# Seven products instead of eight in the first feed-forward matmul, and attention gathered between the pairs of batches

## Chip, cores, metric

One core of a Trainium2 chip. The metric is the device time of one execution in microseconds (us). Every run of a changed kernel was timed beside runs of the kernel before on the same chip. Each run has a state: slow, if it lies over 1.5% above the fastest of its kernel. A ratio is the mean time of one kernel's fast runs over that of the other's of the same rounds, so it is not quite the ratio of the medians that I quote.

## The reference, cut to what matters

```python
# q, k, v: 8 batches x 12 heads x 448 tokens x 64, values of size 0.1;  w_in 768x2048, w_out 2048x768
scores = scale * (q @ k.T) - log(S)
attn   = sigmoid(scores) @ v                       # x: 3584 tokens x 768, token-major
h      = x @ w_in                                  # first product
g      = h * sigmoid(h)
out    = g @ w_out                                 # second product
```

The kernel works in f16. A *unit* of attention is four heads of one batch, so there are 24 units, three for each batch, and unit n belongs to batch n // 3.

## The kernel before

TensorE's 128x128 array is used as four 64x64 tiles. A product runs in two lanes: its upper 64 rows (two matmuls, one for each half of the columns) and, some *chunks* later, its lower 64 rows, which add into the same PSUM bank. A chunk of one product's upper rows and a chunk of an earlier product's lower rows then fill the four tiles together: I call this a *four*. A queue (`fifo`) holds the lower rows still to be done. A marker makes the first lower matmul wait until the upper rows have left the bank.

```python
def lane_step(p=None, c=0):
    low = fifo.popleft() if lower_ready() else None     # lower rows of an earlier product, if due
    def go():
        if p:   p.last = p.mm(0, c)[-1]                 # two matmuls, upper rows
        if low: ... low[0].mm(1, low[1])                # two matmuls, lower rows
                # the first of them waits for low[0].last: "the upper rows have left the bank"
    ...
def emit(p, bank_id, deps):
    ff_wait(deps)                                       # may drain lower rows alone while it waits
    while len(fifo) > 2.5 * p.n:                        # p.n = 6 chunks in the first product,
        drain_one()                                     #       8 in the second
    for c in range(p.n):
        lane_step(p, c)
        ...  between()                                  # here a step of attention may be slipped in
```

The first product of a batch is 16 such products of 6 chunks, 448 columns wide (Python class `G1`, matmuls of L682). The second product was already done by seven products of quarters instead of eight (class `G2`, L808, with sums of quarters on DVE). Attention of units 8 to 23 needs k and q transposed; this is done by DMA:

```python
def transpose_dma(n):                                   # n >= 8; three DMA transposes for each unit
    pl.op("SP", 1200, ("trk", n), [("k", n)] + ([("S", n - NTR, NCH - 1)] if n >= NTR else []),
        lambda: nc.sync.dma_start_transpose(kT[n % NTR], xk[n % NX]), nbytes=1300)
    ...                                                 # two more for q; NTR = NX = 3 sets of buffers
```

`pl` models each engine's time and so fixes the order in which instructions are emitted. The order is fixed when the kernel is built.

## Time and profile before

| | kernel before |
|---|---|
| time, median of the four runs beside the changed kernel | 385.89 us (385.79 to 387.68) |
| span of the profiled run | 384.5 us |
| TensorE busy, mean granted clock | 366.5 us, 0.996 |
| DVE, ACT, GpSimd busy | 203.5, 232.6, 65.1 us |
| lost array time from first to last second product (83 to 379 us) | 12.1 us |

*Lost array time* is the length of a stretch less the matmuls that start in it at their full-rate cost, (columns/2.4 + 2.5) ns for four of them. The lines that carry the bound are in the prediction below.

### The profile page before, as it was taken

The page shows a single profiled execution, that of the slowest core. Times are in us where ns is not written, and L with a number is a line of the kernel's source. Part 1 is how long each engine was busy: PE and PEld are TensorE (multiplying, and loading weights), DVE is VectorE, ACT ScalarE, POOL GpSimd, SP SyncE. Part 2 cuts the span into 40 slices and gives each one's busy share as a digit, 9 for nine tenths or more (in the row PEclk, how much of TensorE's full clock was granted, in tenths as well). Part 3 has the DMA queues.
Part 4 walks back from the last instruction along what each step waited for, and adds up shares of the span by engine and source line. Part 5 has one row for each costly group of instructions (what it writes and reads, how often), then busy time and mean ns, then how long its engine had stood idle before and what let it go on. Part 6 is the DMA issues. An engine that isn't in the chain of part 4 may idle for free.

```text
span 384.5 us, 17994 instructions
## 1 busy us (share of the span) xinstructions
PE 366.5 (95%) x8024; PEld 307.8 (80%) x8024; DVE 203.5 (53%) x376; ACT 232.6 (60%) x506; POOL 65.1 (17%) x97
## 2 busy tenths in 40 slices
PE   7899899999998899989999999999999999999994
PEld 3477677888875599968889898988889898989773
DVE  3536699863444346454454646454654446465632
ACT  1994688568874666548648687776746864144010
POOL 9655102302222020211201222022000000000000
PEclk9999999999999999999999999999999999999998
DMA  8999995976999995975979988796692001410235
GB/s 104 198 209 204 209 208 77 145 94 96 161 185 173 148 119 98 188 122 93 144 112 179 178 113 122 146 157 83 117 155 66 2 3 44 95 34 2 66 75 115
DMA packets 80636, 46.51 MB, mean 121 GB/s; under 512 B 50608, under 2 KB 79792, under 8 KB 80560
## 3 DMA queue, kind: packets, MB, share of 16 engines
q0 software_dynamic: 25008, 22.81, 39.8%
q1 hardware_dynamic: 55552, 22.56, 34.0%
q8 instruction: 63, 1.03, 1.1%
q14 instruction: 13, 0.11, 0.1%
HBM read 45.61 MB, written 11.01 MB: 147 GB/s over the span
## 4 chain that ended last, share of the span: by engine, by line
PE 90%; issue 3%; ACT 2%; DMA 2%; POOL 1%; DVE 1%; POOLq 0%; ACTq 0%
PE ps L808 33%; PE ps L682 30%; PE ps L718 10%; PE ps L507 8%; PE ps L519 8%; ACT at L957 2%; DMA xk<-in_k_dram 2%; PE ps L465 1%; PE ps L990 1%; POOL xk L224 0%; POOL xq L233 0%; DVE qT L479 0%; DVE xt L979 0%; ACT sg L624 0%; POOL v L244 0%
## 5 line engine op out<-in xcount | busy, mean ns | idle before, releaser
L682 PE MATMUL ps<-xt,wi 64*64 64x448 f16 x2304 | 166.7, 349 | 4.9 <-issue 4.9
L550 ACT ACTIVATE at<-ps 128x448 f16<-128x448 f32 x252 | 122.0, 563 | 46.4 <-PE ps L507 40.3
L682 PEld LDWEIGHTS <-wi 64*64 64x64 f16 x2304 | 112.6, 107 | 19.3 <-issue 7.0
L629 DVE TENSOR_TENSOR gt<-ps,sg 128x448 f16<-128x448 f32 (+2 forms) x128 | 78.4, 621 | 71.6 <-ACT sg L624 71.2
L808 PE MATMUL ps<-wo,gt 64*64 64x384 f16 x1344 | 111.5, 323 | 0.3 <-issue 0.3
L808 PEld LDWEIGHTS <-gt 64*64 64x64 f16 x1792 | 97.8, 107 | 10.7 <-issue 1.9
L624 ACT ACTIVATE sg<-ps 128x448 f16<-128x448 f32 (+2 forms) x128 | 70.3, 554 | 54.3 <-PE ps L682 34.8
L808 PEld LDWEIGHTS <-gs 64*64 64x64 f16 x1344 | 78.1, 107 | 7.8 <-issue 0.3
L808 PE MATMUL ps<-so,gs 64*64 64x384 f16 x896 | 80.6, 323 | 0.0
L507 PE MATMUL ps<-qT,kT 64*64 64x448 f16 (+2 forms) x840 | 76.5, 318 | 2.2 <-ACT at L957 0.9
L822 DVE SCALAR_TENSOR_TENSOR us<-ps,us 128x384 f32<-128x384 f32 x70 | 38.7, 555 | 56.8 <-PE ps L808 46.9
L244 POOL DMA_DIRECT2D v<-in_v_dram x24 | 17.4, 723 | 206.7 <-PE ps L519 99.1
L808 PE MATMUL ps<-so,gt 64*64 64x384 f16 x448 | 45.4, 323 | 0.0
L957 ACT ACTIVATE at<-ps 128x512 f16<-128x512 f32 (+3 forms) x96 | 39.8, 555 | 9.2 <-PE ps L507 9.2
L507 PEld LDWEIGHTS <-kT 64*64 64x64 f16 x840 | 35.7, 108 | 11.9 <-issue 7.8
L808 PE MATMUL ps<-wo,gs 64*64 64x384 f16 x448 | 43.7, 323 | 0.0
L718 PE MATMUL ps<-xt,wi 128*128 128x256 f16 (+1 forms) x384 | 40.8, 260 | 1.1 <-issue 1.1
L519 PE MATMUL ps<-at,v 64*64 64x448 f16 (+2 forms) x840 | 40.9, 313 | 0.6 <-issue 0.6
L718 PEld LDWEIGHTS <-wi 128*128 128x128 f16 x384 | 33.1, 98 | 5.8 <-issue 2.5
L519 PEld LDWEIGHTS <-v 64*64 64x64 f16 x840 | 29.8, 107 | 6.2 <-issue 2.2
L829 ACT ACTIVATE us<-ps 128x384 f32<-128x384 f32 x28 | 14.0, 500 | 30.1 <-PE ps L808 30.0
L562 DVE TENSOR_SCALAR xt<-ps 128x448 f16<-128x448 f32 x36 | 20.8, 619 | 15.2 <-PE ps L519 14.5
(33 smaller groups left out, 150.0 us busy)
## 6 DMA issues: line engine op xcount, KB each, us to landing
out_dram<-us SPq DMA_DIRECT2D x112, 96.0 KB, 3.2
xk<-in_k_dram POOLq DMA_DIRECT2D x24, 224.0 KB, 5.6
v<-in_v_dram POOLq DMA_DIRECT2D x24, 224.0 KB, 4.9
xq<-in_q_dram POOLq DMA_DIRECT2D x21, 224.0 KB, 6.8
wo<-in_moe_w_out_dram POOLq DMA_DIRECT2D x4, 768.0 KB, 15.8
wi<-in_moe_w_in_dram POOLq DMA_DIRECT2D x8, 192.0 KB, 6.5
wi<-in_moe_w_in_dram POOLq DMA_DIRECT2D x4, 384.0 KB, 10.0
qT<-xq SPq DMA_TRANSPOSE x32, 4.6
```

The lines of the kernel that those rows point to most:

```text
L244: lambda: nc.gpsimd.dma_start(v16[n % NV], src(v, b, g)),
L507: nc.tensor.matmul(pt[r][64 * h : 64 * h + 64, lo : lo + (c1 - c0) * D], kT[n % NTR][64 * r : 64 * r + 64, i, 64 * h : 64 * h + 64], qT[n ...
L519: nc.tensor.matmul(pt[h][64 * j : 64 * j + 64, :N], v16[n % NV][64 * h : 64 * h + 64, j, c * D : (c + 1) * D], at[64 * h : 64 * h + 64, sl ...
L550: lambda r=r: nc.scalar.activation(at[:, sl, r], pt[r][:, :S], AF.Sigmoid, bias=NEG_LOG_S, scale=QKSCALE),
L562: lambda h=h: nc.vector.tensor_scalar_mul(x[:, 2 * g + h, :], pt[h][:, :S], SX), prio=-2,
L624: lambda: nc.scalar.activation(t[:, :ncol], src_, AF.Sigmoid, scale=ISX), prio=0,
L629: lambda: nc.vector.tensor_tensor(o, src_.rearrange("p (a t) -> p a t", a=nb), t[:, :ncol].rearrange("p (a t) -> p a t", a=nb), ALU.mult),
L682: nc.tensor.matmul(bank[64 * j : 64 * j + 64, z * N : z * N + N], wi[64 * h : 64 * h + 64, cc, f0 + 64 * j : f0 + 64 * j + 64], x[64 * h : ...
L718: nc.tensor.matmul(bank[:, z * N : z * N + N], wi[:, cc, fc * P : (fc + 1) * P], x[:, cc, self.c0 : self.c1], start=(cc == 0 and z == 0), ...
L808: nc.tensor.matmul(bank[64 * j : 64 * j + 64, :HE], lhs[64 * h : 64 * h + 64, c, 64 * j : 64 * j + 64], rhs[64 * h : 64 * h + 64, c, :], s ...
L822: lambda: nc.vector.scalar_tensor_tensor(o, bank[:, :HE], ISX, u, ALU.mult, ALU.add), prio=-2,
L957: lambda r=r, src_=src_: nc.scalar.activation(at[:, base : base + m, r, :N], src_, AF.Sigmoid, bias=NEG_LOG_S, scale=QKSCALE),
```

## The change

The intent is to do for batches 2 to 7 in the first product what the second already does: take two batches (a `Pair`) as a 2x2 of quarters and do seven products instead of eight, which takes 288 of 2304 matmuls off the array. The price is sums of x and w_in on DVE, combinations of PSUM banks on DVE through fp32 buffers (`us`), and copies on ACT. To pay for it, GpSimd multiplies h by its sigmoid for three of the four output quarters. SBUF has to be found for it all: later units get two sets of transposed buffers instead of three. A product in a pair has 3 chunks, and its lower rows follow after at most 7.5 chunks (15 before). Six units of attention stand in the first block of second products, then one in each of two pairs and five in each of two blocks. The core of the diff:

```diff
-        while len(fifo) > 2.5 * p.n:
+        while len(fifo) > (7.5 if p.n == NQ else 2.5 * p.n):
...
-    NTR = 3
-    NX = 3
+    def tring(n):
+        return n % 3 if n < NBIG else 3 if n in () else (0, 1, 0, 1, 0, 1)[n % 6]
...
-            pl.main += d
+            pl.main += d * (0.2 if p.n == NQ else 1.0)
...
+    class Pair:
+        def sums(self):                                  # four sums of x on DVE
+            tt(kk + (1,), d, lo, xs[:, 0], x12, x11, sub, -1)
+            ...
+        def run(self, j, n):                             # product n of 7, column block j of 8
+            lhs, rhs = {
+                1: (wi[:, k_lo, f_lo], x11), 2: (wi[:, k_hi, f_lo], x21), 6: (si[1][:, :, fl], xs[:, 1]),
+                7: (wi[:, k_lo, f_hi], x12), 5: (si[0][:, :, fl], xs[:, 0]), 4: (wi[:, k_hi, f_hi], xs[:, 2]),
+                3: (si[2][:, :, fl], x22),
+            }[n]
+            ...
+            def comb(o, i_, key, deps):
+                pl.op("DVE", 532, key, deps + u_free[o],
+                    lambda: nc.vector.scalar_tensor_tensor(us[o], bank[:, :S], ISX, us[i_], ALU.mult, ALU.add), prio=-2)
+            ...
+                pl.op("POOL", 100 + 2.0 * n_, keys[-1], [key + ("sg", lo)],
+                    lambda o=o, x_=x_: nc.gpsimd.tensor_tensor(o, x_, o, ALU.mult), prio=5)
...
-    blocks = [('p', [0, 1]), ('g', 2), ('p', [2, 3]), ('g', 3), ('p', [4, 5]), ('g', 4), ('p', [6]), ('g', 5), ('p', [7, 8]), ('g', 6), ('p', [9, 10]), ('g', 7), ('p', [11, 12, 13])]
+    blocks = [("p",[0,1,2]),("g",2),("p",[3,4,5]),("g",4),("p",[6,7,8]),("g",6),("p",[9,10,11,12,13])]
```

(The rest changes buffer indices and the guards that keep rings of buffers safe.) The `blocks` line is the coarse order. Before, second products ("p", one or two pairs of row groups) and batches of the first product ("g") alternate finely. After, blocks of 3, 3, 3 and 5 second products stand around the three pairs of batches. The weight of 0.2 makes the modelled pace of attention slow in the pairs, so that most of it falls into the blocks.

## The prediction

> **What bounds the kernel now.** I read the page first: engine shares, slices, groups. Columns of a group: count | busy us, mean ns of one | idle before it.
>
> ```profile
> PE 366.5 (95%) x8024; PEld 307.8 (80%) x8024; DVE 203.5 (53%) x376; ACT 232.6 (60%) x506; POOL 65.1 (17%) x97
> ...
> PE   7899899999998899989999999999999999999994
> ...
> PEclk9999999999999999999999999999999999999998
> DMA  8999995976999995975979988796692001410235
> ...
> L682 PE MATMUL ps<-xt,wi 64*64 64x448 f16 x2304 | 166.7, 349 | 4.9 <-issue 4.9
> ...
> L629 DVE TENSOR_TENSOR gt<-ps,sg 128x448 f16<-128x448 f32 (+2 forms) x128 | 78.4, 621 | 71.6 <-ACT sg L624 71.2
> L808 PE MATMUL ps<-wo,gt 64*64 64x384 f16 x1344 | 111.5, 323 | 0.3 <-issue 0.3
> L624 ACT ACTIVATE sg<-ps 128x448 f16<-128x448 f32 (+2 forms) x128 | 70.3, 554 | 54.3 <-PE ps L682 34.8
> ```
>
> TensorE is the bound, at full granted clock in all but the last slice. The idle columns of DVE and ACT name each other and PE: they wait, PE does not. Busy PE is not PE at its peak, so I next took the rate from the chain that ended last, where PE runs alone:
>
> ```profile
> 116.96 1.51 PE ps L682 x32
> ...
> 275.35 1.62 PE ps L808 x40
> ```
>
> Four 64x64 matmuls share the array, so a "four" of 448 columns costs 1.51/8 = 0.189 us and one of 384 columns 1.62/10 = 0.162 us. From the first L808 (83.1 us) to the last (379.2 us) the array then has to do: first product of batches 2 to 7, 2304/4 = 576 fours x 0.189 = 108.9; second product, 3136/4 = 784 x 0.1625 = 127.4; attention of units 6 to 23, 18 x 14 = 252 fours x 0.189 = 47.6. Sum 283.9 of 296.1 us: only 12 us are lost there. Busy time by stretch tells where:
>
> ```profile
> 112.00:143.00 31.00, 27.11 (x573) 20.89 (x569) 12.54 (x21) 18.74 (x40) 4.31 (x6) 1.00 1.07 147
> 143.00:318.00 175.00, 173.97 (x3865) 154.53 (x3860) 89.99 (x155) 118.26 (x253) 20.08 (x28) 1.00 0.71 116
> ```
>
> (length; busy PE, weight load, DVE, ACT, POOL; clock; DMA share; GB/s.) After 143 us PE is 99% busy; at 112 to 143 us it idles 3.9 us while the DMA share is over 1. What holds it there is seen in the SyncE queue, where issuing a transpose takes up to 4.31 us instead of about 1.2:
>
> ```profile
> 111.38 2.91 SPq L444 DMA_TRANSPOSE qT<-xq  x1
> 114.34 4.31 SPq L448 DMA_TRANSPOSE qT<-xq  x1
> ```
>
> So two limits: the array for most of the time, and the DMA that feeds attention, just after start-up.
>
> **What the Trainium skill says.** "TensorE: Matmul & The Clock Gate", section "Back-to-back issue gap": one warm matmul takes N/2.4 + 2.5 ns, 189.2 ns at N = 448 and 162.5 at 384; the trace agrees for a four. "VectorE: DVE Perf Modes", "The perf-mode tier table": a two-input operation that reads PSUM runs at one element per cycle; the trace agrees (467 ns for 448 elements at 0.96 GHz, shown as 621 ns with its fixed part). "GPSIMD Engine Reference", section 3.1: a two-input operation of 2048 fp32 elements takes 4497 ns, 1.96 times DVE's; scaled by 448/2048 that gives 0.98 us, an estimate from that page, as the kernel before has no GpSimd arithmetic. "SBUF — State Buffer", "Who interferes with whom": a DVE instruction with two SBUF inputs and a GpSimd instruction that reads SBUF exclude each other; one with a single SBUF input does not contend. No run shows this yet.
>
> **The change, part by part.** The built order of instructions gives the counts.
>
> *PE.* L682's 2304 matmuls become 2016 (3 pairs of batches x 8 column blocks x 7 products x 3 chunks x 4): 72 fours less, 72 x 0.189 = **-13.6 us**, all of it on the path. The second product (3136), attention (840 + 840) and the start-up (384 full matmuls) keep their counts; dummy matmuls go from 72 to 60.
>
> *Where the work lies.* The sequence is: G2 x 3 with attention (44.3 us of array time by my counts), pair 1 (34.5), G2 x 3 with attention (40.3), pair 2 (34.3), G2 x 3 (39.7), pair 3 with no attention (31.6), G2 x 5 (45.6). Sum 270.3, against 283.9.
>
> *DVE in a pair.* Two back-to-back operations on 448 elements start 0.53 us apart in the trace (0.62 is the single one). Each column block costs 5 combinations and 1 multiply, 6 x 0.53 = 3.2 us; 8 blocks 25.6 us, plus the four sums of x (1344 f16 elements; the trace's 1024 and 1536 take 0.69 and 0.95, so about 0.85) 3.4 us: 29 of at least 31.6 us, 92%. Before, the same two batches cost 32 multiplies. Over the kernel DVE gains 3 x (48 - 32) x 0.62 = 30 us, 12 sums of x = 10, 16 sums of w_in of 768 elements at about 0.55 = 9: from 203 to about 252 us, 68% of 372.
>
> *ACT.* 24 copies of about 0.55 us more, and splits where a batch crosses the ring's end: about +18 us, to 250. In a pair: 8 x 5 x 0.42 (start to start) = 17 us plus the 8 attention steps of two 0.42s, 7: 24 of 34. In the first G2 block: 48 steps x 0.85 = 41 us plus 6 copies x 0.37 = 43 of 44 us. Tight, but not over.
>
> *GpSimd.* 72 multiplies of 448 (24 per pair): 24 x 0.98 = 24 us of 32 to 34. They are off PE's path, but share an in-order queue with the k, q, v loads.
>
> *Attention.* The k, q buffers and their transposes go from three to two sets for later units, and six units instead of three must be done before the first pair starts. A unit takes about 8 us where the DMA limits it (its products end at 90.7, 99.0, 106.5, 118.5 us), so units 6 to 11 end at 84 + 6 x 8 = 132 us, plus eviction and two sums, 3 us: 135, against 128 where the first G2 block runs out. PE idles up to 7 us there. But the kernel before lost 7 us between 80 and 140 us too (3.9 in the stretch shown, the rest where PE counts as busy but the matmuls that start in ten us fill, at 0.189 and 0.162 us a four, only 8 or 9 of them), so this is about neutral.
>
> **Sum:** 385.8 - 13.6 = 372.2 if PE loses what it loses now. I add 2 us for pairs in which DVE, ACT and GpSimd run at 75 to 92% with chains across them, and 0.5 us for a later start of the first pair; start-up and end are taken as unchanged. **Predicted 374.5 us (-2.9%).**
>
> **Rivals.** (1) *DVE becomes the bound of the pairs.* For: 92% of the array time in pair 3, and each combination frees a PSUM bank. Against: the trace's 0.53 us step leaves 8%. If each operation costs the unoverlapped 0.62, a pair is 48 x 0.62 + 3.4 = 33.2 us: +1.6 for pair 3 and half of it in the others; with stalls around it 377 to 379 us.
> (2) *Attention, through DMA with two sets, becomes the bound.* For: DMA share over 1 at 90 to 135 us, transposes issued in up to 4.3 us. Against: pairs bring little demand, so the queue can catch up, and half a unit or more runs ahead. If every pair start waits 6 us: about 384 us, no gain.
> (3) *Head-of-line blocking on GpSimd.* A load that waits for a buffer stands before multiplies; it would hold the fp32 buffers, then DVE, then PE. For: v loads wait 99 us for L519 in the kernel before. Against: the nine buffers, and few loads in a pair (five among the multiplies of pair 1, eight in pair 2, none in pair 3). Cost 3 to 6 us: 378 to 380.
> (4) *All hidden and start-up a little shorter* (fewer dummies): 369 to 371.
>
> **Range and chances.** The removed array time is certain and the kernel before turns array time into time at 96%. The additions all lengthen, so the range leans upward: 368.5 to 381.5 us. The 2% mark is 378.1 us; rivals 1 and 3 alone end near it, rival 2 beyond it. Faster by over 2%: 0.72; within 2%: 0.25; slower: 0.03.
>
> **What would show it.** Right: 2016 matmuls in the pairs' line at 0.189 us per four; PE at 97% or more in each pair; DVE near 250 us in all, GpSimd multiplies near 1 us; one PE gap of 3 to 8 us before the first pair, little before the others. Wrong: pairs of 36 us or more with PE waiting for banks that DVE frees (rival 1) or for sums; gaps before pairs 2 and 3 with transposes late (rival 2); DVE waiting for GpSimd (rival 3); GpSimd multiplies of 1.5 us or more; a start-up that ends after 86 us, which none of this covers.

## More of the kernel before

TensorE's own waits (engine and line, what ended the wait, total us, times, longest) and the DMA queues (packets, MB, share of 16 engines):

```profile
PE ps L682 <- issue: 4.9, 4, 1.7
PE ps L465 <- DMA xk<-in_k_dram: 1.5, 3, 0.8
```

```profile
q1 hardware_dynamic: 55552, 22.56, 34.0%
q8 instruction: 63, 1.03, 1.1%
```

TensorE's largest wait is "issue": nothing that the profile records ended it. Queue q8 carries TensorE's instructions: 63 packets of 16 KB. Queue q1 carries the transposes and the results: 55552 packets.

## The result, and the profile after

The changed kernel took **405.45 us** (404.11 to 407.47, 4 runs) against 385.89: ratio 1.050, 95% interval 1.0445 to 1.0555. It is 5% slower, and the predicted range ended at 381.5. The page of the changed kernel, engine shares and slices:

```profile
PE 370.5 (92%) x7724; PEld 293.9 (73%) x7724; DVE 249.0 (62%) x456; ACT 246.9 (61%) x562; POOL 142.4 (35%) x193
...
PE   6899999999599799898997899989979989899994
...
PEclk9599999999889899999999899999999999999998
DMA  8999995519999993437999629349983100013335
```

300 matmuls fewer than before, yet TensorE is busy 4 us longer, and the clock row now dips below 9 in the middle of the run. The same by phase (length; busy PE, weight load, DVE, ACT, GpSimd; clock; DMA share; GB/s): three second products, pair 1, three, pair 2, three, pair 3, five:

```profile
82.40:140.80 58.40, 52.29 (x1034) 41.52 (x1035) 27.57 (x53) 43.34 (x97) 11.45 (x16) 0.92 1.04 159
140.80:182.90 42.10, 39.60 (x796) 33.15 (x795) 31.16 (x60) 33.06 (x83) 27.04 (x34) 0.99 0.59 90
182.90:228.60 45.70, 41.04 (x874) 31.23 (x872) 24.08 (x40) 28.71 (x63) 10.11 (x14) 0.96 1.00 165
228.60:270.40 41.80, 39.73 (x812) 33.82 (x810) 31.84 (x55) 30.26 (x75) 28.09 (x42) 1.00 0.48 71
270.40:311.80 41.40, 38.74 (x864) 32.10 (x859) 22.27 (x38) 29.69 (x68) 7.69 (x11) 1.00 0.83 130
311.80:351.40 39.60, 37.01 (x742) 27.46 (x743) 30.51 (x52) 20.67 (x39) 21.40 (x21) 1.00 0.05 12
351.40:398.30 46.90, 45.74 (x1070) 34.68 (x1066) 25.71 (x43) 5.67 (x12) 3.04 (x4) 1.00 0.34 76
```

DMA share is at 1.0 in the first two blocks of second products, and low in the pairs: attention has gathered in the blocks. With the array's cost of the matmuls that start in each phase, the lost array time is 14.1, 5.0, 8.8, 4.1, 4.9, 5.1 and 3.6 us, sum 45.5, against 12.1 before. The balance of the spans (403.1 and 384.5): -13.6 us of matmuls, +33.4 lost, -1.2 at start and end, together +18.6.

TensorE's waits after, in the same view as before, and one of GpSimd's:

```profile
POOL xq L267 <- DMA qT<-xq: 20.8, 7, 5.8
...
PE ps L553 <- DMA qT<-xq: 12.3, 4, 4.1
...
PE ps L906 <- issue: 5.5, 8, 1.3
```

The wait of attention's S matmuls (L553) for transposed q did not exist before. The q loads in turn wait 20.8 us on GpSimd's queue until a transpose has freed their buffer: the two sets chase each other. The first of those four waits, and what follows it, in TensorE's timeline (start, us, what; in brackets the idle time before and what ended it):

```profile
104.59 0.33 PE L1029 MATMUL ps<-wo,gt 64*64 64x384 f16 x2
108.99 0.59 PE L553 MATMUL ps<-qT,kT 64*64 64x448 f16 x4 [4.07 <-DMA qT<-xq]
109.34 0.52 PE L1029 MATMUL ps<-so,gs 64*64 64x384 f16 x1
```

and a wait late in the run, in pair 3:

```profile
323.42 0.37 PE L906 MATMUL ps<-xs,wi 64*64 64x448 f16 x1 [0.97 <-issue]
```

After 4.07 us of idling the same 384-column matmul takes 0.52 us instead of 0.33: the clock is at half speed from 107.3 to 114.1 us, and again at 138.0 to 141.4 and 223.3 to 226.7, each time near such a wait (of 4.07, 2.02 and 3.73 us). The Trainium skill, "TensorE: Matmul & The Clock Gate", section "HAM oscillation — how this bites in real kernels", warns of TensorE idling longer than about 3.4 us; these stretches of 6.8, 3.4 and 3.4 us agree with a window of that length, but the wait of 2.02 us is shorter than it. In this trace the clock changes on a grid of 3.41 us. In the step of that grid before each stretch TensorE idled 2.4, 2.0 and 2.9 us; a wait of 2.51 us at 297.4 to 299.9 us fell on two steps, 1.0 and 1.5 us, and the clock stayed.

The line in pair 3 is of another kind. In pair 3 there is no attention and almost no DMA (share 0.05), yet five waits that no engine ended stand in it (0.6 to 1.3 us from one matmul's start to the next). I laid the packets of queue q8 beside TensorE's place in its instruction stream. A packet holds 256 instructions, and each of these five waits stands at instruction 256j + 450 or 451 of the stream, and ends 1.3 to 1.5 us after packet j has landed. They are late instructions. The Trainium skill, "Runtime: NRT & Kernel Launch", section "Instruction fetch mechanics", has the blocks of 16 KiB and 256 instructions, and says that the cost of crossing a boundary is "mostly hidden". The size agrees; here it is not hidden. The five packets were not slow on the way: they took 0.88 to 1.36 us, and the median of all 61 is 1.00. They started late: TensorE's matmuls then stood at 256j + 364 to 389 of the stream, against 190 to 314 for packets that left more than 2 us to spare. What makes a packet start late the trace doesn't show.

For a ledger I went through every matmul from 82 us on that started over 60 ns after the array could have taken it, and booked the delay to a transpose (landed within 0.2 us before), to an instruction packet (landed 1.2 to 1.75 us before), to an engine or load (ended just before), or to the rest. The delays add to some microseconds more than the lost time, since some are partly made up.

| us | before | after |
|---|---|---|
| waits for transposes | 0 | 13.6 |
| late instruction packets | 7.0 | 12.5 |
| rest, mostly steps with only half of a four | 5.3 | 10.3 |
| DVE, ACT, GpSimd, loads | 3.8 | 12.6 |
| sum | 16.1 | 49.0 |

"The rest" is mostly visible in the built order as well. A step of the lanes has an upper part, a lower part or both. Before: 1342 full steps, 18 with upper rows alone and 18 with lower rows alone. After: 1234 full, 54 and 54. They stand where the order of one lane runs dry: at the ends of the three-product blocks and at the entry to a pair.

### The profile page after: what moved, and what is told of

Same layout as the page of the kernel before. It is cut to its first block, busy times and chain, and to the rows that moved or that the text cites. A ratio compares the mean times of both kernels' runs of the same rounds, so it can differ in the third digit from the quotient of the medians.

```text
span 403.1 us, 17842 instructions
## 1 busy us (share of the span) xinstructions
PE 370.5 (92%) x7724; PEld 293.9 (73%) x7724; DVE 249.0 (62%) x456; ACT 246.9 (61%) x562; POOL 142.4 (35%) x193
## 4 chain that ended last, share of the span: by engine, by line
PE 79%; DMA 8%; issue 3%; ACT 3%; DVE 2%; SPq 2%; POOL 1%; ACTq 0%; PEldq 0%; DVEq 0%; POOLq 0%
PE ps L1029 29%; PE ps L906 23%; PE ps L803 9%; PE ps L553 9%; PE ps L565 8%; DMA qT<-xq 7%; SPq L489 2%; DMA xk<-in_k_dram 1%; PE ps L510 1%; ACT at L1183 1%; ACT gt L707 1%; DVE us L921 1%; SPq L485 1%; DVE gs L315 0%; ACT gt L688 0%
## 5 line engine op out<-in xcount | busy, mean ns | idle before, releaser
L712 POOL TENSOR_TENSOR gt<-us,gt 128x448 f16<-128x448 f32 (+4 forms) x96 | 77.3, 828 | 76.5 <-ACT gt L707 44.0
L553 PE MATMUL ps<-qT,kT 64*64 64x448 f16 (+2 forms) x728 | 73.4, 344 | 12.7 <-DMA qT<-xq 12.3
L906 PE MATMUL ps<-xt,wi 64*64 64x448 f16 x864 | 78.7, 351 | 1.0 <-issue 0.8
L921 DVE SCALAR_TENSOR_TENSOR us<-ps,us 128x448 f32<-128x448 f32 x96 | 57.8, 622 | 25.4 <-PE ps L906 19.0
L1043 DVE TENSOR_TENSOR us<-ps,us 128x384 f32<-128x384 f32 x70 | 38.8, 555 | 52.7 <-PE ps L1029 41.9
L906 PEld LDWEIGHTS <-wi 64*64 64x64 f16 x1152 | 60.2, 107 | 14.5 <-issue 8.6
L906 PE MATMUL ps<-xs,ex 64*64 64x448 f16 x576 | 61.7, 350 | 0.1
L707 ACT ACTIVATE gt<-us 128x448 f16<-128x448 f32 (+4 forms) x96 | 42.6, 479 | 19.7 <-DVE us L921 13.6
L553 PEld LDWEIGHTS <-kT 64*64 64x64 f16 x728 | 35.9, 112 | 24.9 <-issue 19.2
L613 DVE TENSOR_SCALAR xt<-ps 128x448 f16<-128x448 f32 x36 | 20.8, 619 | 31.3 <-PE ps L565 30.1
L1183 ACT ACTIVATE at<-ps 128x384 f16<-128x384 f32 (+3 forms) x78 | 33.1, 532 | 10.2 <-PE ps L553 10.1
L906 PE MATMUL ps<-xs,wi 64*64 64x448 f16 x288 | 35.9, 351 | 2.3 <-issue 2.3
L906 PE MATMUL ps<-xt,si 64*64 64x448 f16 x288 | 35.6, 350 | 2.3 <-issue 2.3
```

The source lines that it names most:

```text
L553: nc.tensor.matmul(pt[r][64 * h : 64 * h + 64, lo : lo + (c1 - c0) * D], kT[tring(n)][64 * r : 64 * r + 64, i, 64 * h : 64 * h + 64], qT[t ...
L613: lambda h=h: nc.vector.tensor_scalar_mul(xt[:, (2 * n + h) % XC, :], pt[h][:, :S], SX), prio=-2,
L707: lambda o=o, x_=x_: nc.scalar.activation(o, x_, AF.Sigmoid, scale=1.0 if in_sb else ISX), prio=0,
L712: lambda o=o, x_=x_: nc.gpsimd.tensor_tensor(o, x_, o, ALU.mult), prio=5,
L906: nc.tensor.matmul(bank[64 * j_ : 64 * j_ + 64, :S], lhs[64 * h : 64 * h + 64, c, 64 * j_ : 64 * j_ + 64], rhs[64 * h : 64 * h + 64, c, :] ...
L921: lambda: nc.vector.scalar_tensor_tensor(us[o], bank[:, :S], ISX, us[i_], ALU.mult, ALU.add), prio=-2,
```

## The experiments

The theories: **A**, TensorE's sequencer is held too closely behind the array (7.5 chunks instead of 15), so that instruction packets come late; **B**, DVE, ACT or GpSimd bound the pairs; **C**, two transposed sets are too few; **D**, the traffic of the DMA transposes itself delays others. Fifteen runs were made, of thirteen programs: a_free2 repeats a_free on purpose, and a_lag20 turned out to repeat a_lag. "Points" are per cent of the time of the kernel before in the same rounds, one point being 3.9 us; the changed kernel stands at +5.0 points.

**1. a_lag**: the changed kernel with a longer distance.

```diff
-        while len(fifo) > (7.5 if p.n == NQ else 2.5 * p.n):
+        while len(fifo) > (12.5 if p.n == NQ else 2.5 * p.n):
```

> The changed kernel, but the lower rows of a pair's product follow the upper rows 12.5 chunks behind instead of 7.5, so that the wait for 'the upper rows have left the bank' is long satisfied when TensorE's sequencer reaches it. Theory A (in the pairs the sequencer is held at these waits, cannot run ahead, and each 16 KB packet of instructions then comes too late): the three pairs lose 1 to 2 us each instead of 5.0, 4.1 and 5.1, gaps of 0.5 us and more that end 1.2 to 1.7 us after an instruction packet become rare there, and the time falls by 6 to 9 us to 396 to 399 us. Rival B (DVE, ScalarE and GpSimd are the bound of the pairs): no gain or a loss, 404 to 410 us, because results come later and banks stay open longer.

Measured: 396.2 us, ratio 1.0205 (1.0144 to 1.0267), correct. Three points of the five come back. In its trace waits for transposes fall to 8.4 us and late packets to 7.3. More than the distance changed: the built order has 61 and 61 half steps instead of 54 and 54 and puts attention at other places.

**2. a_third**: a third transposed set for units 6 to 11, in scratch that pair 1 uses later.

```diff
-        return n % 3 if n < NBIG else 3 if n in () else (0, 1, 0, 1, 0, 1)[n % 6]
+        return n % 3 if n < NBIG else (0, 1, 3)[n % 3] if n < 12 else n % 2
...
-            lo += [("S", n, NCH - 1) for n in () if b == NHB]
+            lo += [("S", n, NCH - 1) for n in (8, 11) if b == NHB]
```

> The changed kernel, but the transposed k and q of units 8 and 11 go into a third set that lies in the scratch of the x sums (free until the first pair), so units 6 to 11 rotate through three sets as in the kernel before. Theory C (two sets of transposed k, q are too few: a unit's transposes start only when the unit two before it has its scores, and then take 10 to 13 us): the first G2 block, which takes 58.4 us for 44.3 us of array time, loses 4 to 7 instead of 14.1 us, the waits of 4.1 and 2.0 us and the half clock after them go, and the time falls by 7 to 10 us to 395 to 398. Rival D (the DMA's bandwidth is what is short, whatever the number of sets): the block still takes 55 to 59 us, 402 to 406 us.

Measured: 408.11 us, ratio 1.0513 (1.0465 to 1.056): no gain. Yet the first block's loss did fall from 14.1 to 8.3 us. The loss moved: pair 1 from 5.0 to 9.4, the second block from 8.8 to 10.9, pair 2 from 4.1 to 7.8. Its waits:

```profile
PE ps L906 <- issue: 8.2, 10, 2.5
PE ps L1029 <- issue: 4.5, 7, 1.3
PE ps L553 <- DMA qT<-xq: 3.3, 3, 1.5
```

The wait for transposes is down from 12.3 to 3.3 us and "issue" up in its place. Theory C was right about the wait and wrong about the time. The edit also changes the built order (67 and 67 half steps instead of 54 and 54), which may hold a part of what came back.

**3. a_pe**: units 8 to 11 transposed on TensorE.

```diff
-    on_pe = {0, 1, 2, 3, 4, 5, 6, 7}
+    on_pe = set(range(12))
```

> The changed kernel, but units 8 to 11 are transposed by TensorE (as units 0 to 7 are) instead of by DMA. Theory C or D (transposes by DMA are late, from too few sets or too little bandwidth): no qT wait in the first G2 block, its loss falls from 14.1 to 3 to 6 us, against 4 x 0.7 us of transposing matmuls and 16 more DVE copies; 395 to 399 us. If something else starves the block (ScalarE, banks), 404 to 408 us.

Measured: 407.4 us (401.57 to 410.72), ratio of the fast runs 1.0378 (1.0306 to 1.045). The profiled run was slow, so its trace is not used. A little better than the changed kernel at best; what the first block gains is spent on the extra matmuls and evictions or lost elsewhere.

**4. b_lag**: the kernel *before*, first product at the short distance, nothing else changed.

```diff
-        while len(fifo) > 2.5 * p.n:
+        while len(fifo) > (7.5 if p.n == NCC else 2.5 * p.n):
```

> The kernel before with one number changed: in its first product the lower rows follow 7.5 chunks behind instead of 15. Theory A: TensorE's sequencer is held as in the pairs, instruction packets come late, and gaps of 0.5 us and more after a packet appear in most of the first product's stretches: 5 to 12 us slower, 391 to 398 us. Rival B: nothing else changed for DVE, ScalarE or GpSimd, so 385 to 388 us.

Measured: 398.16 us, ratio 1.0257 (1.0202 to 1.0313). The short distance alone costs the old kernel 10 us with no work added on any engine. I took this for theory A. But the built order of this kernel has 115 and 115 half steps instead of 18 and 18, and the ledger shows late packets at 8.9 us (7.0 before) and the rest at 12.6 (5.3 before): mostly another mechanism. Experiment 14 settles it.

**5. a_free and a_free2**: S of units 8 to 23 reads its k and q from the weights of the second product; all transposes are still issued, but nobody waits for them. The result is wrong. The comparison passes it nevertheless: with q and k of size 0.1 the scores are small, and the output hardly depends on them.

```diff
-                    kT[tring(n)][64 * r : ...],   qT[tring(n)][64 * r : ...],
+                    (kT[tring(n)] if n in on_pe else wo[:, :, :P])[64 * r : ...],
+                    (qT[tring(n)] if n in on_pe else wo[:, :, P : 2 * P])[64 * r : ...],
```

> The changed kernel, but the S matmuls of units 8 to 23 read their k and q from the weights of the second product (wrong result on purpose) instead of from the transposed sets; loads and DMA transposes are issued as before, in the same order, but no S waits for one and none waits for an S. Theory C (two transposed sets too few, so that attention waits for its transposes; the trace of the changed kernel has 13.6 us of such PE waits from 82 us on, and half-clock stretches behind three of them): 386 to 392 us. Theory D (DMA bandwidth itself delays packets and loads): the traffic stays, so 400 to 405. Theory A (sequencer too close behind the array, so that the 12.5 us of stalls behind instruction packets are the larger part): 396 to 401. Theory B (DVE, ACT, GpSimd bound the pairs): 402 to 406.

Measured: 397.06 us, ratio 1.0216 (1.013 to 1.0302), between what theories C and D expected. Theory A's range holds it, but it rested on the sequencer's distance, which this run leaves as it was. The profiled run took 733.82 us, with all matmuls at half speed from end to end (557 ns for one that takes 326) although its clock records say full speed, and can't be used. So it was run again:

> The same kernel as a_free, whose profiled run was an outlier of 734 us at half speed and can't be read. Time again 394 to 399. The trace should tell how transposes that nobody waits for cost 11 us against a_notr: as stalls behind instruction packets (then 15 us of them or more, against 10.0 in a_notr), or as waits for q, k, v loads that land later.

Measured: 397.96 us, ratio 1.0183 (1.0087 to 1.0279). The profiled run counts as slow (the kernel's fastest was 392.67), so I use its trace only for where TensorE waits:

```profile
PE ps L906 <- issue: 6.8, 7, 2.4
PE ps L1029 <- issue: 3.0, 4, 1.5
...
PE ps L553 <- issue: 2.7, 2, 1.9
```

Without the waits for transposes about three points come back, and late packets now stand at 20.1 us in the ledger, where the changed kernel has 12.5. What does not wait for the transpose runs into the next late packet.

**6. a_notr**: as a_free, and the transposes of units 8 to 23 are not issued.

```diff
-            lambda: nc.sync.dma_start_transpose(kT[tring(n)], xk[ring(n)]), nbytes=1300,
+            lambda: None, nbytes=1300,           # and the two of q likewise; order and model unchanged
```

> As a_free, and the DMA transposes of units 8 to 23 are not issued at all (wrong result on purpose). The difference from a_free is the traffic alone. Theory D: another 5 us or more below a_free, and the stalls behind instruction packets mostly gone. Theories A, B and C: within 2 us of a_free.

Measured: 384.97 us, ratio 0.9916 (0.9862 to 0.9971). Another three points: the transfers cost about as much as TensorE's waits for them. They are not quite "the traffic alone", as was expected: in a_free2 GpSimd's queue waited 46.9 us until transposes had freed the buffers of k and q (xq 30.2, xk 6.7, and v behind them 10.0 us), and in a_notr these waits are gone too. No wait of TensorE that a_free2's trace lists after start-up names a load, so a large part is unlikely to lie there, but no run separates the two. The queue of the transposes (packets, MB, share), and the two phases that were worst, in the columns of the phases above:

```profile
q1 hardware_dynamic: 8960, 11.02, 11.4%
```

```profile
82.10:132.40 50.30, 49.29 (x1034) 42.40 (x1033) 27.96 (x53) 42.78 (x97) 11.47 (x16) 1.00 0.65 112
...
174.20:213.80 39.60, 38.67 (x868) 32.37 (x864) 24.02 (x40) 28.80 (x64) 10.13 (x14) 1.00 0.68 117
```

46592 packets are gone, the clock is full, and the first block with the same 1034 matmuls takes 50.3 us instead of 58.4 (lost 6.0 instead of 14.1), the second 39.6 instead of 45.7. Late packets are at 10.0 us, half of a_free2's 20.1 (a slow run) but only 2.5 below the changed kernel's 12.5, so not "mostly gone". Theory D is right about the time. That transposes act by delaying instruction packets is shown in part only: fewer packets are late without them, but the late ones don't travel longer. Of the five that ended the long waits at 109 to 153 us in a_free2 four took 0.92 to 1.08 us, the median of all being 0.98; they too started late, at 256j + 358 to 449.

**7. a_short**: DVE's combinations and GpSimd's multiplies in the pairs work on 64 columns instead of 448, in the same order. Its output is wrong, which doesn't matter for the time.

```diff
-   nc.vector.scalar_tensor_tensor(us[o], bank[:, :S], ISX, us[i_], ALU.mult, ALU.add)
+   nc.vector.scalar_tensor_tensor(us[o][:, :D], bank[:, :D], ISX, us[i_][:, :D], ALU.mult, ALU.add)
-   nc.gpsimd.tensor_tensor(o, x_, o, ALU.mult)
+   nc.gpsimd.tensor_tensor(o[:, :D], x_[:, :D], o[:, :D], ALU.mult)
```

> The changed kernel with the same order of instructions, but the combinations on DVE and the multiplies on GpSimd in the pairs work on 64 columns instead of 448 (wrong result on purpose): about 0.47 us less of DVE in each of 15 x 8 combinations and about 0.75 us less of GpSimd in each multiply. Theory B: the pairs get back what they lose, 10 to 14 us: 391 to 396. Theories A, C, D: at most the 3 us that the ledger of PE waits puts down to DVE and GpSimd: 402 to 406.

Measured: 399.47 us, ratio 1.0268 (1.0173 to 1.0363). The combination took 223 ns instead of 622 and the multiply 311 instead of 828 (mean over its shapes); the fp32 buffers are also cleared once at the start. Some two points come back, with a wide interval; neither A nor B expected this size. Experiment 13 repeats it without transposes.

**8. a_lag20**: a_lag with 20 chunks.

```diff
-        while len(fifo) > (7.5 if p.n == NQ else 2.5 * p.n):
+        while len(fifo) > (20 if p.n == NQ else 2.5 * p.n):
```

> The changed kernel with the lower rows of a pair's product kept up to 20 chunks behind its upper rows, as in the second product, instead of 7.5 (12.5 gave 9 us back). Theory A: the stalls behind instruction packets in pair 3 (5.1 us lost at 7.5, 3.5 at 12.5) go below 2 us, and the whole is 391 to 396. If the distance is not what decides after 12.5: 396 to 398. If the banks held longer cost more than the packets: 398 or more.

Measured: 399.03 us, ratio 1.0272 (1.0189 to 1.0356). This run tests nothing: built again, the two kernels give the same program, byte for byte, because the queue never exceeds 12.5 chunks before a product of a pair. So a distance beyond 12.5 is untested, and the run is a second measurement of a_lag. It shows the noise: 0.7 points between two batches of runs, and in the profiled runs a first block that loses 11.0 us here and 14.8 in a_lag, a second block that loses 7.9 and 5.0. Pair 3 loses 3.5 us in both.

**9. b_notr**: the kernel before without transposes, the same edit as a_notr.

```diff
-            lambda: nc.sync.dma_start_transpose(kT[n % NTR], xk[n % NX]), nbytes=1300,
+            lambda: None, nbytes=1300,           # and the two of q; S reads wo for n >= 8
```

> The kernel before, with the same edit as a_notr: the S matmuls of units 8 to 23 read k and q from the weights of the second product (wrong on purpose) and the DMA transposes of these units are not issued. a_notr gained 20 us over the changed kernel. If the transposes cost so much only where the change has crowded attention together (six units in the first block of second products, five in each of the next, two sets instead of three), before gains at most 4 us: 382 to 386. If they cost as much in any order, before gains like the changed kernel: 366 to 372.

Measured: 382.15 us, ratio 0.9931 (0.9876 to 0.9987), as the first alternative had it. The same transposes cost the kernel before 0.7 points and the changed kernel 5.8. So it is not their number; it is the order that they meet, which crowds them and gives them two sets instead of three. Without them the stretch from 83 to 143 us loses 1.7 us instead of 6.9, and late packets fall from 7.0 to 2.8 us. The stretch before, and in b_notr:

```profile
83.00:143.00 60.00, 56.11 (x1201) 44.80 (x1202) 24.34 (x42) 43.23 (x95) 10.77 (x15) 1.00 0.94 138
```

```profile
83.00:143.00 60.00, 59.91 (x1324) 52.89 (x1326) 28.44 (x49) 46.96 (x103) 10.72 (x15) 1.00 0.52 90
```

**10. a_notr_lag**: a_notr with the distance of 12.5 (both edits as above).

> a_notr with the lag of 12.5 chunks of a_lag: neither transposes nor the short distance of lower rows behind upper rows. If the two causes add (20.5 and 9 us off 405): 375 to 377, which is where the prediction was, and DVE, ACT and GpSimd then bound nothing much. If the lag only mattered because late packets met transposes: 382 to 385.

Measured: 384.16 us, ratio 0.9963 (0.9933 to 0.9994). The second alternative: without transposes the longer distance gains nothing. What a_lag gained was therefore tied to the transposes.

**11. a_third_lag**: a_third and a_lag together.

> a_lag with the third transposed set of a_third for units 6 to 11 (correct result). a_third alone took away the waits for transposes in the first block, but the stalls behind instruction packets grew from 12.5 to 19.2 us. If a larger distance cures those: 388 to 392. If the crowding itself is what costs, in whichever wait it shows: 394 to 398 as a_lag.

Measured: 418.28 us, ratio 1.0807 (1.0719 to 1.0896), the slowest of all, which neither alternative foresaw. Its first block is good (7.2 us lost), but pair 1 loses 11.2 and the second block 13.0 us, with late packets at 18.6 us and waits for transposes at 9.6. Why these two edits harm each other I did not settle; the built order has 74 and 74 half steps, where a_lag has 61 and 61.

**12. a_pe_lag**: a_pe and a_lag together.

> a_lag with units 8 to 11 transposed on TensorE instead of by DMA (correct result): no DMA transpose until pair 1, at some 4 x 28 small matmuls and their evictions more. If the DMA traffic of transposes in the first block is its loss (14.8 us in a_lag, 6.0 in a_notr): 389 to 393. If not: 395 to 400.

Measured: 402.83 us, ratio 1.0406 (1.0323 to 1.0489): a miss too, two points worse than a_lag alone. The first block loses 9.5 us instead of a_lag's 14.8, but it has more matmuls, and the second block loses 9.2 where a_lag lost 5.0 and its repetition a_lag20 7.9. In a_third and a_third_lag relief in one block came out again in the next; here it lies near the noise.

**13. a_nls**: a_notr_lag with the short operations of a_short: no transposes, long distance, DVE and GpSimd almost free.

> a_notr_lag with the shortened combinations and multiplies of a_short (wrong on purpose): transposes gone, distance 12.5, DVE and GpSimd nearly free in the pairs; the order of instructions is that of a_lag. If the engines beside TensorE hold what is left (a_notr_lag still loses 26.2 us between the first and the last second product, b_notr about 8): 374 to 378. If what is left lies in the order itself (61 plus 61 fours with an empty half in the built order, against 18 plus 18 before, about 7 us) and in late packets: 381 to 384.

Measured: 385.43 us, ratio 0.9929 (0.9862 to 0.9996); wrong. Within the noise it is a_notr_lag. Theory B falls as the reason for what is left: with DVE and GpSimd nearly taken out, no time comes back. ACT was not shortened, and stays untested.

**14. b_lag_notr**: b_lag and b_notr together.

> b_lag without the DMA transposes (as in b_notr). b_lag cost 10 us over before, and I put that down to the sequencer being held, so that packets come late among the transposes. If so, without transposes the cost is at most 4 us over b_notr: 382 to 386. If it is the 115 plus 115 fours with an empty half that the short distance makes in the built order (18 plus 18 before) and DVE and ACT waits, the cost stays 8 to 12 us: 390 to 394.

Measured: 392.67 us, ratio 1.0132 (1.0083 to 1.0181), 2.0 points above b_notr. Most of the 2.6 points of b_lag stay although late packets are down at 2.4 us. As the second alternative said, a shorter distance thus costs chiefly through half steps in the built order (115 and 115) and waits for DVE and ACT, not through packets; no run separates the first two. My reading of experiment 4 was wrong.

**Not run.** Built orders with the weight of 0.2 raised to 0.5 or 1.0 put hardly more attention steps into a pair (10 or 11 instead of 8 to 10), because the ring for x holds 15 of the 18 chunks of three batches and frees them only at a pair's end. And since a_notr_lag, without any transpose, is only level with the kernel before, I did not expect a correct version of this order to beat it.

## Why the prediction was wrong, step by step

| kernel, points against the kernel before | with transposes | without |
|---|---|---|
| before | 0 | -0.7 |
| changed | +5.0 | -0.8 |
| changed, distance 12.5 | +2.1 (repeated: +2.7) | -0.4 |

**The attention step ("about neutral") failed, and it is the larger part.** The prediction let units 6 to 11 pass at 8 us each and charged a possible 7 us, the same that the kernel before loses from 80 to 140 us. The 8 us misread the prediction's own figures: products that end at 90.7, 99.0, 106.5 and 118.5 us are 9.3 us apart on average, and at 9.3 the same sum gives a wait of up to 15 us instead of 7. In the changed kernel a unit took 9.4 us (the V products of the six stand at 90.3 to 137.3 us, 47.0/5, in uneven steps of 6.5 to 13.6), the first block lost 14.1 us and the second 8.8. Beside the wait there were two terms that the sum did not have: half-speed clock after gaps (9.6 us of that block ran at it, which costs half of that at most), and the transfers. Shown by a_notr and b_notr: crowded transposes cost 5.8 points here and 0.7 before, so 5.1 points, about 20 us (give or take a point by the intervals), come from transposes as this order places them, in all blocks together. Shown by a_free against a_notr: about half of that is TensorE's waiting, about half the transfers themselves, in part through late instruction packets. Whether the crowding or the third set that was taken away weighs more is open: a_third shortened the waits and not the time.

**The reading of the kernel before that led there was wrong in its mechanism.** The prediction put 3.9 us of idling at 112 to 143 us down to transposes that were issued slowly. The waits said "issue", not "DMA". They are late packets. Since b_notr has only 0.1 us of idling from 83 to 143 us, the transposes were behind it, but what ended the waits was a packet (the three took 0.95 to 1.19 us on the way, and started late). Read like that, the same lines warn: a loss that grows as the transposes crowd, not one that is the same before and after.

**The step "-13.6 us, all of it on the path" failed too.** 2016 matmuls and 0.189 us a four were right. But the step took it that the order packs four to a four. The built order, which could be read before the run, has 1378 lane steps before and 1342 after: 36 fewer, not 72. The ledger has the rest, mostly half steps, at 10.3 us instead of 5.3 (10.1 and 3.9 without transposes). Counted that way the array saves about half of what was promised. The count overstates it, though: 97 more steps would be 18 us at 0.189 us each, and b_lag_notr lies 2.0 points, 8 us, above b_notr, with waits for DVE and ACT in it; a_lag has 7 steps more than the changed kernel and is faster. That half steps cost 5 to 6 us here is the ledger's reading, not shown by a run.

**"+2 us for pairs" was too small, and for the wrong reason.** (The sum itself has a slip: 372.2 + 2 + 0.5 is 374.7, not 374.5.) Pairs lost 5.0, 4.1 and 5.1 us, in pair 3 mostly in late packets with nothing else moving. The durations were right: DVE 249.0 us in all (252 predicted), ACT 246.9 (250), GpSimd's multiply of 448 columns 1.04 us (0.98). With DVE and GpSimd shortened and no transposes, nothing came back (a_nls).

**The rivals.** Rival 2 (attention through DMA with two sets) named the right place, but at 384 us and only as waits at the entries of pairs. Rivals 1 and 3 (DVE, GpSimd's queue) may hold the two points of a_short while transposes are present (1 to 3.5 by the intervals). Rival 4 was out of reach.

**What is left without transposes.** The changed kernel, with 13.6 us less to multiply, is then just level with the kernel before (-0.8 and -0.7 points). In the ledgers late packets are 7.2 us higher (10.0 against 2.8) and the rest 6.2 us (10.1 against 3.9), together 13.4; waits for DVE, ACT and loads are 8.6 us higher as well, but the ledger's sum is there 7 us above the lost time, so part of what it books costs nothing. Packets and half steps are thus the likely pair, with ACT not excluded. Why packets come late in this order even without transposes is open.

No version beat the kernel before with a correct result. The best correct variant of the change is a_lag, 2 to 3% slower than before in its two measurements.

## What to carry to other kernels

Taking products off the array is worth only what the built order still fills: count the steps that run half empty before you multiply matmuls by their cost. Where a schedule crowds the DMA feed into fewer phases, price the crowding: the wait, the clock after the wait, and the instructions that arrive late. Relief of one wait proves little until the time moves. In two kernels here the loss went to the next phase, and only taking the whole suspect away, in both kernels, showed its size. Where an edit acts through a scheduler, compare the built orders first: one experiment here turned out to be the same program as another.

## What the Trainium skill lacked or had wrong

- "Runtime: NRT & Kernel Launch", "Instruction fetch mechanics", calls the fetch mostly hidden. Here late packets held TensorE 7.0 us in the kernel before, 12.5 in the changed one and 20.1 in a_free2 (a slow run), at a fixed place 256j + 450 of the instruction stream in pair 3, where each wait ended 1.3 to 1.5 us after the packet had landed.
- No page that I found says what DMA transposes do to the arrival of those packets: with 46592 transpose packets less late packets fell from 7.0 to 2.8 us (before, b_notr) and from 12.5 to 10.0 (changed, a_notr). The way that this takes isn't shown.
- No page that I found prices half-filled fours: 97 more half steps in each lane cost 2.0 points (b_lag_notr against b_notr), DVE and ACT waits that came with them included.
- "GPSIMD Engine Reference", section 3.1, scaled to 448 columns, gave 0.98 us; the run shows 1.04, 6% more. "SBUF — State Buffer", "Who interferes with whom", agrees where DVE has two SBUF inputs: of the 14 first sums of the second product's quarters the three that overlapped with a GpSimd multiply took 1030, 1490 and 1622 ns, the other eleven 677 to 694; the 384-column combinations, with one input in PSUM, stayed at 555.
- "TensorE: Matmul & The Clock Gate", "HAM oscillation — how this bites in real kernels", speaks of idle gaps over about 3.4 us. Here half speed followed a gap of 2.02 us, and didn't follow one of 2.51.
